# A six-layer cross network on one core: later loads issued layer by layer, the prologue's products reordered, one small weight load moved to GpSimd and small loads issued ahead of GpSimd's own work

## The chip, the cores and the metric

The kernel runs on one core of one Trainium2 chip. The metric is the device time of one execution in microseconds (us).

## The reference

The input x0 has 4096 rows and 416 columns (bf16); there are six layers, each with a 416x416 weight and a bias.

```python
B, F, D, L = 4096, 26, 16, 6          # Din = F * D = 416
def reference(x0, ws, bs):
    x = x0
    for l in range(ws.shape[0]):
        x = x0 * (x @ ws[l] + bs[l]) + x
    return x
```

Every layer multiplies by x0 and adds x. So x after l layers is x0 times a sum that can be kept in TensorE's accumulator banks: the kernel never clears them between layers, and adds a running sum of the biases ("bias sums").

## The kernel before

The 416 columns are three chunks of 128 and a tail of 32. The rows run in four blocks of 1024, the columns on the partitions, so x0 has to come in transposed. For the first block TensorE transposes most of it itself: rows 0 to 511 with transposes, rows 512 to 767 (the "third input block") and the 32 tail columns ("tail inputs") with products by an identity that GpSimd builds. Rows 768 to 1023 come by a transposing DMA. All of this is the prologue. Layer 0 of block 0 multiplies the first two chunks (k=0, k=1), then runs the third input block, the tail inputs and the bias sums, then k=2, and then the "tail rows": products whose contraction is the 32 tail columns, part 0 and part 1 (part 1 also uses the "corner" weights, tail columns by tail columns). After that each layer repeats the same pattern without any setup work.

Loads, and GpSimd's share:

```python
        IN_BANKS = ((3, 4, 6), (0, 5, 7))
        IN_ORDER = ((0, 0), (1, 0), (0, 1), (1, 1), (0, 2), (1, 2))
        THIRD = (6, 7, 3)
        HALVES = (slice(0, 64), slice(64, 128))
        # ... (cut)
        def load_wt(eng, g, a, b, done):
            n0, n1 = ((0, 256), (256, DF))[g % 2]
            eng.dma_start(
                wt_sb[lane(g), a:b, 0:n1 - n0], ws[a:b, DF:D, n0:n1].rearrange("l p n -> p l n")
            ).then_inc(done, 16)
        # ... (cut)
        @block.sync
        def _(sp):
            sp.dma_start(xin_sb[:, 0:2, :], x0_v[:, 0:2, :]).then_inc(s_xin[0], 16)
            sp.dma_start(w_sb[:, 0, 0, :], ws[0, 0:128, :]).then_inc(s_w0, 16)
            sp.dma_start(xin_sb[:, 4:6, :], x0_v[:, 4:6, :]).then_inc(s_xin[2], 16)
            load_wt(sp, 0, 0, 1, s_wt[0])
            sp.dma_start_transpose(x0T_sb[:, :, 768:SB], x0[768:SB, 0:DF]).then_inc(s_x0T[0], 16)
            for l in range(1, L):
                sp.dma_start(w_sb[:, l, :, :], wmain(l)).then_inc(s_w[l], 16)
                if l == 1:
                    for g in range(4):
                        load_wt(sp, g, 1, L, s_wt[1])
        # ... (cut)
            for s in range(1, NS):
                sp.dma_start_transpose(
                    x0T_sb[:, :, s * SB:(s + 1) * SB], x0[s * SB:(s + 1) * SB, 0:DF]
                ).then_inc(s_x0T[s], 16)
                sp.dma_start_transpose(
                    x4_sb[:, s - 1:s, :], x0[s * SB:(s + 1) * SB, D - 128:D]
                ).then_inc(s_x4[s - 1], 16)
            for s in range(NS - 1):
                n = (s + 1) * L
                sp.wait_ge(s_xa, NC * n)
                sp.wait_ge(s_xb, NC * n)
                for c in range(NC):
                    sp.dma_start_transpose(
                        o_sb[:, s * JS:(s + 1) * JS, c * 128:(c + 1) * 128], xo_sb[:, s, c, :]
                    ).then_inc(s_oT, 16)
                sp.wait_ge(s_xt, n)
                sp.dma_start_transpose(ot_sb[:, s, :, :], xot_sb[:, s, :]).then_inc(s_ot, 16)
                sp.wait_ge(s_oT, 16 * NC * (s + 1))
                sp.wait_ge(s_otc, s + 1)
                sp.dma_start(
                    out_v[:, s * JS:(s + 1) * JS, :], o_sb[:, s * JS:(s + 1) * JS, :]
                ).then_inc(s_out, 16)
        # ... (cut)
        @block.gpsimd
        def _(pool):
            pool.memset(ones_sb[:, :], 1.0).then_inc(s_ones, 1)
            pool.dma_start(bsa_sb[1:L + 1, :], bs[:, :]).then_inc(s_bs, 16)
            pool.wait_ge(s_ones, 1)
            pool.affine_select(
                out=ident[:, :], in_=ones_sb[:, 0:128], pattern=[[-1, 128]],
                compare_op=ALU.is_equal, fill=0.0, base=0, channel_multiplier=1,
            ).then_inc(s_set, 1)
            pool.affine_select(
                out=u_sb[:, :], in_=ones_sb[0:L + 1, 0:L], pattern=[[1, L]],
                compare_op=ALU.is_ge, fill=0.0, base=1, channel_multiplier=-1,
            ).then_inc(s_set, 1)
            load_wt(pool, 2, 0, 1, s_wtp)
            pool.wait_ge(s_zero, 1)
            for i, (a, b) in enumerate(((0, 1), (1, L))):
                for g in (1, 3):
                    pool.dma_start(
                        wc_sb[lane(g), a:b, 32 * g:32 * g + 32], ws[a:b, DF:D, DF:D].rearrange("l p n -> p l n")
                    ).then_inc(s_wc[i], 16)

        # ... (cut)
                    if l == 1 and s > 0:
                        pool.wait_ge(s_ot, 16 * s)
                        pool.tensor_copy(
                            out=o_sb[:, (s - 1) * JS:s * JS, DF:D].rearrange("p (g r) f -> p r g f", r=2),
                            in_=ot_sb[:, s - 1, :, :].rearrange("p r (g f) -> p r g f", f=DR),
                        ).then_inc(s_otc, 1)
        # ... (cut)
            def tail_inputs():
                for r in range(2):
                    for g in range(4):
                        for i in range(2):
                            j = 2 * (g ^ i) + r
                            src = xin_sb[:, j, DF:D] if j < 6 else xtl_sb[:, j - 6, :]
                            ins = tile_mm(ps[lane(g), 5 - i, r * 128:r * 128 + 128], src, ident[:, :], g, True)
                ins.then_inc(s_tp, 1)

            def third_input():
                pe.wait_ge(s_xin[2], 16)
                pe.wait_ge(s_inD, 4)
                for c in range(NC):
                    for j in range(2):
                        for q in range(4):
                            f0 = c * 128 + 32 * q
                            ins = tile_mm(
                                ps[lane(q), THIRD[c], j * 128:j * 128 + 128], xin_sb[:, 4 + j, f0:f0 + 32], ident[:, :], q, True
                            )
                    ins.then_inc(s_inT, 1)

            fill(14)
```

The order of the first layer on TensorE, and the copies out of its banks on VectorE (dve) and ScalarE (act):

```python
            def bias_sums():
                pe.wait_ge(s_bs, 16)
                pe.wait_ge(s_zero, 2)
                pe.wait_ge(s_set, 2)
                pe.wait_ge(s_inD, 5)
                for c in range(NC + 1):
                    for q in range(4):
                        f0 = c * 128 + 32 * q if c < NC else DF
                        ins = tile_mm(ps[lane(q), 6, c * 8:c * 8 + L], bsa_sb[:, f0:f0 + 32], u_sb[:, :], q, True)
                ins.then_inc(s_cbp, 1)
        # ... (cut)
                    if n == 0:
                        pe.wait_ge(s_w0, 16)
                        for k in range(NC):
                            if k == 1:
                                pe.wait_ge(s_w[0], 16)
                            if k == 2:
                                third_input()
                                pe.wait_ge(s_xtl0, 16)
                                tail_inputs()
                                bias_sums()
                            before_a(k)
                            for m in range(NC):
                                step(m, 0, k)
                    else:
                        if s == 0:
                            pe.wait_ge(s_w[l], 16)
                        chunk(0, 0, before_a)
                        chunk(1, 0)
                        chunk(2, 0)

                    if n == 0:
                        pe.wait_ge(s_inD, 6)
                        pe.wait_ge(s_inA, 3)
                        pe.wait_ge(s_te, 1)
                        pe.wait_ge(s_te0, 1)
                    else:
                        pe.wait_ge(s_xb, NC * n)
                        if l == 0:
                            pe.wait_ge(s_xt, n)
                            pe.wait_ge(s_te, s + 1)
                        else:
                            pe.wait_ge(s_sw, s * (L - 1) + l)
                    if s == 0 and l < 2:
                        if l == 1:
                            pe.wait_ge(s_wc[1], 32)
                        pe.wait_ge(s_wt[l], (48, 64)[l])
                    if n == 0:
                        pe.wait_ge(s_wtp, 16)

        # ... (cut)
                    lo, hi = slice(0, G), slice(G, 2 * G)
                    for part in range(2):
                        if n == 0 and part == 1:
                            pe.wait_ge(s_cb, 1)
                            pe.wait_ge(s_wc[0], 32)
                        for h in range(2):
                            g, wm = 2 * h, slice(part * 128, part * 128 + 128)
                            row(g, ps[:, NC * h + part, :], wt_sb[lane(g), l, wm], slice(0, H), h == 1)
                            g += 1
        # ... (cut)
                            else:
                                row(g, ps[:, 6 + h, lo], wc_sb[lane(g), l, 0:128], lo, True)
                        for h in range(2):
                            g = 2 * h + 1
                            if part == 1:
                                ins = row(g, ps[:, 6 + h, lo], wc_sb[lane(g), l, 32:160], hi, False)
                    ins.then_inc(s_ti, 1)
                    if n == 0:
                        pe.wait_ge(s_x0T[0], 16)
        # ... (cut)
            for c in (0, 2):
                dve.wait_ge(s_inT, 2 * NC + c + 1)
                dve.tensor_copy(out=x0T_sb[:, c, 512:768], in_=ps[:, THIRD[c], 0:G]).then_inc(s_inD, 1)
            dve.wait_ge(s_tp, 1)
            dve.tensor_copy(out=x0t_sb[:, 0, G:2 * G], in_=ps[:, 4, 0:G]).then_inc(s_te0, 1)
            dve.wait_ge(s_cb, 1)
        # ... (cut)
            act.wait_ge(s_inT, 2 * NC + 2)
            act.activation(out=x0T_sb[:, 1, 512:768], in_=ps[:, THIRD[1], 0:G], func=ACTF.Copy).then_inc(s_inA, 1)
            def swap_lanes(buf, done):
                for g in range(4):
                    ins = act.activation(out=buf[lane(g), G:2 * G], in_=buf[lane(g ^ 1), 0:G], func=ACTF.Copy)
                ins.then_inc(done, 1)

            act.wait_ge(s_tp, 1)
            act.activation(out=x0t_sb[:, 0, 0:G], in_=ps[:, 5, 0:G], func=ACTF.Copy).then_inc(s_te, 1)
            act.wait_ge(s_cbp, 1)
            act.activation(
                out=cb_sb[:, :, :],
                in_=ps[:, 6, 0:8 * (NC + 1)].rearrange("p (c e) -> p c e", e=8)[:, :, 0:L], func=ACTF.Copy,
            ).then_inc(s_cb, 1)
            act.wait_ge(s_cb, 1)
```

## Time and profile before

| | before |
|---|---|
| median device time | 130.58 us (3 runs, 130.36 to 130.84) |
| profiled span | 129.4 us |
| TensorE busy | 124.6 us, 96% |
| pitch of two layers in the chain of waits | 4.87 us, all 24 layers alike |
| layer 0's tail rows start (the end of the prologue) | 8.88 us |

In all lines of the profile PE is TensorE, PEld its weight loads, DVE VectorE, ACT ScalarE, POOL GpSimd and SP SyncE. L342 is source line 342, xN a count, and "issue" is time in which an engine waited for nothing that the profile shows.

From the chain of waits of before (start us, length us, what):

```profile
4.03 1.39 PE ps L240 x12
5.42 1.91 PE ps L201 x29
...
7.36 0.43 DVE x0T_sb L426
...
7.93 1.02 PE ps L201 x28
8.95 0.32 PE ps L342
...
9.49 4.33 PE ps L201 x84
```

Up to the end of the last layer the chain is TensorE's own work but for one piece: at 7.36 it is a VectorE copy. The piece of 4.33 us that starts at 9.49 is the body of layer 0, and it is followed by the next tail rows at 13.82, one layer pitch later.

From the timeline of before (start us, length us, engine, line, operation, and in brackets the idle time before it and what ended it):

```profile
1.38 0.72 POOL L159 DMA_DIRECT2D bsa_sb<-in_bs_dram  x1 [0.26 <-issue]
...
2.18 0.32 POOL L161 TENSOR_SCALAR_AFFINE_SELECT ident<-ones_sb 128x128 bf16<-128x128 bf16 x1
...
3.96 1.46 PE L240 MATMUL ps<-ident,xin_sb 128*128 128x128 bf16 x12
...
7.36 0.76 DVE L426 CAST x0T_sb<-ps 128x256 bf16<-128x256 f32 x2 [1.61 <-PE ps L201]
...
7.93 0.26 PE L201 MATMUL ps<-u_sb,bsa_sb 7*32 7x6 bf16 x16 [0.18 <-DVE x0T_sb L426]
...
8.88 0.39 PE L342 MATMUL ps<-x0t_sb,wt_sb 32*128 32x512 bf16 x1
...
9.42 2.45 PE L201 MATMUL ps<-x0T_sb,w_sb 128*32 128x256 bf16 x48
```

GpSimd starts the identity right after its first DMA issue, at 2.18. TensorE's bias sums stood still for 0.18 us because they write bank 6, from which VectorE was still copying the third input block.

### The profile page before, as it was taken

The page shows a single profiled execution, that of the slowest core. Times are in us where ns is not written, and L with a number is a line of the kernel's source. Part 1 is how long each engine was busy: PE and PEld are TensorE (multiplying, and loading weights), DVE is VectorE, ACT ScalarE, POOL GpSimd, SP SyncE. Part 2 cuts the span into 40 slices and gives each one's busy share as a digit, 9 for nine tenths or more (in the row PEclk, how much of TensorE's full clock was granted, in tenths as well). Part 3 has the DMA queues.
Part 4 walks back from the last instruction along what each step waited for, and adds up shares of the span by engine and source line. Part 5 has one row for each costly group of instructions (what it writes and reads, how often), then busy time and mean ns, then how long its engine had stood idle before and what let it go on. Part 6 is the DMA issues. An engine that isn't in the chain of part 4 may idle for free.

```text
span 129.4 us, 5407 instructions
## 1 busy us (share of the span) xinstructions
PE 124.6 (96%) x2448; PEld 62.7 (48%) x2448; DVE 100.3 (78%) x154; ACT 71.4 (55%) x164; POOL 22.7 (18%) x41
## 2 busy tenths in 40 slices
PE   7999999999999999999999999999999999999980
PEld 6655445445445445445445445445445445445450
DVE  2339779779779779779779779779789789789790
ACT  0626456476746456475745555575755555555680
POOL 7602012012012022012012022022022032022130
PEclk9999999999999999999999999999999999999999
DMA  3999999898007708000008944000009834000025
GB/s 107 295 264 318 124 194 174 177 120 181 0 10 126 143 0 268 0 0 5 5 0 159 110 136 133 5 0 0 5 0 115 154 129 139 5 0 5 0 85 186
DMA packets 32934, 12.54 MB, mean 97 GB/s; under 512 B 25338, under 2 KB 32912, under 8 KB 32912
## 3 DMA queue, kind: packets, MB, share of 16 engines
q1 hardware_dynamic: 31536, 11.49, 44.0%
q10 hardware_dynamic: 1184, 0.67, 1.7%
q8 instruction: 19, 0.31, 1.0%
q0 software_dynamic: 192, 0.05, 0.2%
q14 instruction: 3, 0.02, 0.1%
HBM read 2.90 MB, written 3.41 MB: 49 GB/s over the span
## 4 chain that ended last, share of the span: by engine, by line
PE 96%; DVE 1%; issue 0%; DVEq 0%
PE ps L201 84%; PE ps L342 10%; PE ps L240 1%; DVE o_sb L451 1%; PE ps L395 0%; DVE x0T_sb L426 0%; DVEq L33 0%; PE ps L357 0%
## 5 line engine op out<-in xcount | busy, mean ns | idle before, releaser
L446 DVE SCALAR_TENSOR_TENSOR xT_sb<-ps,cb_sb,x0T_sb 128x512 bf16<-128x512 f32 x120 | 80.9, 743 | 16.9 <-PE ps L342 16.9
L201 PE MATMUL ps<-xT_sb,w_sb 128*32 128x512 bf16 (+1 forms) x1680 | 89.0, 364 | 0.0
L201 PEld LDWEIGHTS ps<-xT_sb,w_sb 128*32 128x32 bf16 x1680 | 43.0, 97 | 38.7 <-issue 4.2
L475 ACT ACTIVATE xt_sb<-xt_sb 32x256 bf16<-32x256 bf16 x80 | 33.1, 414 | 16.6 <-POOL xt_sb L188 15.9
L498 ACT ACTIVATE t_sb<-ps,cb_sb 64x256 f32<-64x256 f32 x48 | 22.5, 469 | 30.5 <-PE ps L201 30.2
L188 POOL TENSOR_TENSOR xt_sb<-t_sb,x0t_sb 128x256 bf16<-128x256 f32 x20 | 13.4, 672 | 83.0 <-ACT t_sb L498 83.0
L201 PE MATMUL ps<-x0T_sb,w_sb 128*32 128x512 bf16 (+1 forms) x336 | 18.8, 369 | 0.0
L446 DVE SCALAR_TENSOR_TENSOR xo_sb<-ps,cb_sb,x0T_sb 128x512 bf16<-128x512 f32 x23 | 15.6, 744 | 3.4 <-PE ps L342 3.3
L201 PEld LDWEIGHTS ps<-x0T_sb,w_sb 128*32 128x32 bf16 x336 | 8.5, 98 | 7.9 <-issue 1.6
L342 PE MATMUL ps<-xt_sb,wt_sb 32*128 32x512 bf16 x80 | 12.1, 379 | 0.0
L511 ACT ACTIVATE x0t_sb<-x_sb 32x256 bf16<-32x256 bf16 x24 | 9.9, 413 | 0.4
L357 PE MATMUL ps<-xt_sb,wt_sb 32*128 32x512 bf16 x40 | 7.8, 385 | 0.0
L342 PE MATMUL ps<-xt_sb,wc_sb 32*128 32x256 bf16 x80 | 7.7, 268 | 0.0
L342 PEld LDWEIGHTS ps<-xt_sb,wt_sb 32*128 32x128 bf16 x80 | 2.3, 92 | 8.5 <-DVE xT_sb L446 8.5
L342 PEld LDWEIGHTS ps<-xt_sb,wc_sb 32*128 32x128 bf16 x80 | 4.0, 93 | 2.3
L188 POOL TENSOR_TENSOR xot_sb<-t_sb,x0t_sb 128x256 bf16<-128x256 f32 x4 | 2.7, 671 | 12.6 <-ACT t_sb L498 12.6
L201 PE MATMUL ps<-const-bfloat16-1.0 128*32 128x256 bf16 x56 | 3.2, 419 | 0.8 <-PEq L548 0.8
L421 DVE COPY x0T_sb<-ps 128x256 bf16<-128x256 bf16 x4 | 1.0, 292 | 2.9 <-PE ps L240 2.9
L468 ACT ACT_TABLE_LOAD x1 | 1.3, 1283 | 3.4 <-issue 3.4
L201 PEld LDWEIGHTS ps<-const-bfloat16-1.0 128*32 128x32 bf16 x56 | 2.4, 144 | 1.2 <-issue 0.8
L342 PE MATMUL ps<-x0t_sb,wt_sb 32*128 32x512 bf16 x16 | 2.4, 380 | 0.0
L173 POOL DMA_DIRECT2D wc_sb<-in_ws_dram x4 | 2.2, 554 | 0.0
(45 smaller groups left out, 28.8 us busy)
## 6 DMA issues: line engine op xcount, KB each, us to landing
out_dram<-o_sb SPq DMA_DIRECT2D x3, 832.0 KB, 4.1
w_sb<-in_ws_dram SPq DMA_DIRECT2D x5, 312.0 KB, 4.5
xin_sb<-in_x_dram SPq DMA_DIRECT2D x2, 208.0 KB, 3.5
out_dram<-o_sb SPq DMA_DIRECT2D x1, 256.0 KB, 2.3
xin_sb<-in_x_dram ACTq DMA_DIRECT2D x1, 208.0 KB, 3.2
w_sb<-in_ws_dram ACTq DMA_DIRECT2D x1, 208.0 KB, 3.9
out_dram<-o_sb SPq DMA_DIRECT2D x1, 208.0 KB, 2.3
out_dram<-o_sb ACTq DMA_DIRECT2D x1, 208.0 KB, 2.7
```

Of the source, the lines that this page charges most:

```text
L173: pool.dma_start(wc_sb[lane(g), a:b, 32 * g:32 * g + 32], ws[a:b, DF:D, DF:D].rearrange("l p n -> p l n")).then_inc(s_wc[i], 16)
L188: pool.tensor_tensor(out=dst, in0=t32_sb[:, n % 2, :], in1=x0t_sb[:, s, 0:G], op=ALU.mult).then_inc(s_xt, 1)
L201: return pe.matmul(dst, lhsT=lhsT, rhs=rhs, start=start, stop=True, skip_group_check=True, tile_position=(0, 32 * q),)
L240: ins = pe.transpose(out=psT[:, IN_BANKS[h][c], (j % 2) * 128:(j % 2 + 1) * 128], in_=xin_sb[:, j, c * 128:(c + 1) * 128], identity=ident[ ...
L342: return pe.matmul(dst, lhsT=lhsT, rhs=srct[lane(g), cols], start=l == 0 and start, stop=True, skip_group_check=True, tile_position=(32 * ...
L357: pe.matmul(ps[:, NC * h + 2, :], lhsT=wt_sb[lane(g), l, 0:128], rhs=srct[lane(g), :].rearrange("p (b r) -> p b r", b=2)[:, ::-1, :], star ...
L446: dve.scalar_tensor_tensor(out=dst, in0=ps[:, NC * half + c, :], scalar=cb_sb[:, c, l:l + 1], in1=x0T_sb[:, c, o:o + H], op0=ALU.add, op1= ...
L451: dve.tensor_copy(out=o_sb[:, j0 + 4:j0 + 8, 0:256], in_=psT[:, 4, :].rearrange("p (j d) -> p j d", d=256)).then_inc(s_oeD, 1)
L468: act.activation(out=x0T_sb[:, 1, h * 256:(h + 1) * 256], in_=psT[:, IN_BANKS[h][1], 0:256], func=ACTF.Copy).then_inc(s_inA, 1)
L475: ins = act.activation(out=buf[lane(g), G:2 * G], in_=buf[lane(g ^ 1), 0:G], func=ACTF.Copy)
L498: ins = act.activation(out=t32_sb[HALVES[h], n % 2, :], in_=tail(h), func=ACTF.Identity, bias=cb_sb[HALVES[h], NC, l:l + 1],)
L511: ins = act.activation(out=x0t_sb[lane(g), s + 1, swap * G:(swap + 1) * G], in_=x4_sb[96:128, s, r * G:(r + 1) * G], func=ACTF.Copy,)
```

## The change

It has four intents. (1) The bias sums go into bank 4, which is free, so that they need not wait. (2) The tail inputs go ahead of the third input block, both halves into one bank, so that one ScalarE copy replaces a ScalarE and a VectorE copy; the copy of the bias sums goes from ScalarE to VectorE, and some waits of the first tail rows move to part 1. (3) One tail weight moves from SyncE to GpSimd, and GpSimd issues it, the other tail weight and one corner weight before it builds the identity. (4) Weights of layers 2 to 5 are issued as the layers proceed, and the transposed rows of later blocks one block at a time.

```diff
-        THIRD = (6, 7, 3)
+        THIRD = (3, 6, 7)
# ... (cut)
 
         @block.sync
         def _(sp):
+            def load_rows(s):
+                sp.dma_start_transpose(
+                    x4_sb[:, s - 1:s, :], x0[s * SB:(s + 1) * SB, D - 128:D]
+                ).then_inc(s_x4[s - 1], 16)
+                sp.dma_start_transpose(
+                    x0T_sb[:, :, s * SB:(s + 1) * SB], x0[s * SB:(s + 1) * SB, 0:DF]
+                ).then_inc(s_x0T[s], 16)
+
             sp.dma_start(xin_sb[:, 0:2, :], x0_v[:, 0:2, :]).then_inc(s_xin[0], 16)
             sp.dma_start(w_sb[:, 0, 0, :], ws[0, 0:128, :]).then_inc(s_w0, 16)
             sp.dma_start(xin_sb[:, 4:6, :], x0_v[:, 4:6, :]).then_inc(s_xin[2], 16)
-            load_wt(sp, 0, 0, 1, s_wt[0])
             sp.dma_start_transpose(x0T_sb[:, :, 768:SB], x0[768:SB, 0:DF]).then_inc(s_x0T[0], 16)
             for l in range(1, L):
+                if l > 1:
+                    sp.wait_ge(s_ti, (1, 2, 2, 2)[l - 2])
+                if l == L - 1:
+                    load_rows(1)
                 sp.dma_start(w_sb[:, l, :, :], wmain(l)).then_inc(s_w[l], 16)
                 if l == 1:
                     for g in range(4):
                         load_wt(sp, g, 1, L, s_wt[1])
-            for s in range(1, NS):
-                sp.dma_start_transpose(
-                    x0T_sb[:, :, s * SB:(s + 1) * SB], x0[s * SB:(s + 1) * SB, 0:DF]
-                ).then_inc(s_x0T[s], 16)
-                sp.dma_start_transpose(
-                    x4_sb[:, s - 1:s, :], x0[s * SB:(s + 1) * SB, D - 128:D]
-                ).then_inc(s_x4[s - 1], 16)
             for s in range(NS - 1):
                 n = (s + 1) * L
                 sp.wait_ge(s_xa, NC * n)
@@ -137,6 +141,8 @@
                     ).then_inc(s_oT, 16)
                 sp.wait_ge(s_xt, n)
                 sp.dma_start_transpose(ot_sb[:, s, :, :], xot_sb[:, s, :]).then_inc(s_ot, 16)
+                if s < NS - 2:
+                    load_rows(s + 2)
                 sp.wait_ge(s_oT, 16 * NC * (s + 1))
                 sp.wait_ge(s_otc, s + 1)
                 sp.dma_start(
@@ -157,6 +163,16 @@
         def _(pool):
             pool.memset(ones_sb[:, :], 1.0).then_inc(s_ones, 1)
             pool.dma_start(bsa_sb[1:L + 1, :], bs[:, :]).then_inc(s_bs, 16)
+            for g in (0, 2):
+                load_wt(pool, g, 0, 1, s_wtp)
+            def load_wc(i, g):
+                a, b = ((0, 1), (1, L))[i]
+                pool.dma_start(
+                    wc_sb[lane(g), a:b, 32 * g:32 * g + 32], ws[a:b, DF:D, DF:D].rearrange("l p n -> p l n")
+                ).then_inc(s_wc[i], 16)
+
+            pool.wait_ge(s_zero, 1)
+            load_wc(0, 1)
             pool.wait_ge(s_ones, 1)
             pool.affine_select(
                 out=ident[:, :], in_=ones_sb[:, 0:128], pattern=[[-1, 128]],
@@ -166,13 +182,9 @@
                 out=u_sb[:, :], in_=ones_sb[0:L + 1, 0:L], pattern=[[1, L]],
                 compare_op=ALU.is_ge, fill=0.0, base=1, channel_multiplier=-1,
             ).then_inc(s_set, 1)
-            load_wt(pool, 2, 0, 1, s_wtp)
-            pool.wait_ge(s_zero, 1)
-            for i, (a, b) in enumerate(((0, 1), (1, L))):
-                for g in (1, 3):
-                    pool.dma_start(
-                        wc_sb[lane(g), a:b, 32 * g:32 * g + 32], ws[a:b, DF:D, DF:D].rearrange("l p n -> p l n")
-                    ).then_inc(s_wc[i], 16)
+            load_wc(0, 3)
+            for g in (1, 3):
+                load_wc(1, g)
 
             for s in range(NS):
# ... (cut: the copy of the stored tail moves from layer 1 to layer 2 of the next row block)
                             j = 2 * (g ^ i) + r
                             src = xin_sb[:, j, DF:D] if j < 6 else xtl_sb[:, j - 6, :]
-                            ins = tile_mm(ps[lane(g), 5 - i, r * 128:r * 128 + 128], src, ident[:, :], g, True)
+                            ins = tile_mm(ps[lane(g), 5, i * G + r * 128:i * G + r * 128 + 128], src, ident[:, :], g, True)
                 ins.then_inc(s_tp, 1)
 
             def third_input():
-                pe.wait_ge(s_xin[2], 16)
# ... (cut)
                 pe.wait_ge(s_bs, 16)
                 pe.wait_ge(s_zero, 2)
                 pe.wait_ge(s_set, 2)
-                pe.wait_ge(s_inD, 5)
                 for c in range(NC + 1):
                     for q in range(4):
                         f0 = c * 128 + 32 * q if c < NC else DF
-                        ins = tile_mm(ps[lane(q), 6, c * 8:c * 8 + L], bsa_sb[:, f0:f0 + 32], u_sb[:, :], q, True)
+                        ins = tile_mm(ps[lane(q), 4, c * 8:c * 8 + L], bsa_sb[:, f0:f0 + 32], u_sb[:, :], q, True)
                 ins.then_inc(s_cbp, 1)
# ... (cut)
                             if k == 1:
                                 pe.wait_ge(s_w[0], 16)
                             if k == 2:
-                                third_input()
+                                bias_sums()
+                                pe.wait_ge(s_xin[2], 16)
                                 pe.wait_ge(s_xtl0, 16)
                                 tail_inputs()
-                                bias_sums()
+                                third_input()
                             before_a(k)
                             for m in range(NC):
                                 step(m, 0, k)
@@ -320,10 +331,9 @@
                         chunk(2, 0)
 
                     if n == 0:
-                        pe.wait_ge(s_inD, 6)
-                        pe.wait_ge(s_inA, 3)
+                        pe.wait_ge(s_inD, 5)
                         pe.wait_ge(s_te, 1)
-                        pe.wait_ge(s_te0, 1)
+                        pe.wait_ge(s_cb, 1)
                     else:
                         pe.wait_ge(s_xb, NC * n)
                         if l == 0:
@@ -334,9 +344,9 @@
                     if s == 0 and l < 2:
                         if l == 1:
                             pe.wait_ge(s_wc[1], 32)
-                        pe.wait_ge(s_wt[l], (48, 64)[l])
+                        pe.wait_ge(s_wt[l], (32, 64)[l])
                     if n == 0:
-                        pe.wait_ge(s_wtp, 16)
+                        pe.wait_ge(s_wtp, 32)
# ... (cut)
                     lo, hi = slice(0, G), slice(G, 2 * G)
                     for part in range(2):
                         if n == 0 and part == 1:
-                            pe.wait_ge(s_cb, 1)
+                            pe.wait_ge(s_inD, 6)
+                            pe.wait_ge(s_inA, 3)
                             pe.wait_ge(s_wc[0], 32)
# ... (cut)
+            dve.wait_ge(s_cbp, 1)
+            dve.tensor_copy(
+                out=cb_sb[:, :, :], in_=ps[:, 4, 0:8 * (NC + 1)].rearrange("p (c e) -> p c e", e=8)[:, :, 0:L],
+            ).then_inc(s_cb, 1)
             for c in (0, 2):
                 dve.wait_ge(s_inT, 2 * NC + c + 1)
                 dve.tensor_copy(out=x0T_sb[:, c, 512:768], in_=ps[:, THIRD[c], 0:G]).then_inc(s_inD, 1)
-            dve.wait_ge(s_tp, 1)
-            dve.tensor_copy(out=x0t_sb[:, 0, G:2 * G], in_=ps[:, 4, 0:G]).then_inc(s_te0, 1)
             dve.wait_ge(s_cb, 1)
# ... (cut)
-            act.wait_ge(s_inT, 2 * NC + 2)
-            act.activation(out=x0T_sb[:, 1, 512:768], in_=ps[:, THIRD[1], 0:G], func=ACTF.Copy).then_inc(s_inA, 1)
             def swap_lanes(buf, done):
                 for g in range(4):
                     ins = act.activation(out=buf[lane(g), G:2 * G], in_=buf[lane(g ^ 1), 0:G], func=ACTF.Copy)
                 ins.then_inc(done, 1)
 
             act.wait_ge(s_tp, 1)
-            act.activation(out=x0t_sb[:, 0, 0:G], in_=ps[:, 5, 0:G], func=ACTF.Copy).then_inc(s_te, 1)
-            act.wait_ge(s_cbp, 1)
-            act.activation(
-                out=cb_sb[:, :, :],
-                in_=ps[:, 6, 0:8 * (NC + 1)].rearrange("p (c e) -> p c e", e=8)[:, :, 0:L], func=ACTF.Copy,
-            ).then_inc(s_cb, 1)
+            act.activation(out=x0t_sb[:, 0, :], in_=ps[:, 5, :], func=ACTF.Copy).then_inc(s_te, 1)
+            act.wait_ge(s_inT, 2 * NC + 2)
+            act.activation(out=x0T_sb[:, 1, 512:768], in_=ps[:, THIRD[1], 0:G], func=ACTF.Copy).then_inc(s_inA, 1)
             act.wait_ge(s_cb, 1)
```

## The prediction

> **What bounds the kernel now.** The page gives TensorE busy 124.6 of 129.4 us (96%); the chain of waits is TensorE for 96%. In that chain successive layers' tail-row groups start 4.87 us apart, all 24 layers (13.82, 18.69, 23.56 ... 121.00), in stretches with a DMA share of 1.25 as of 0.15 (windows view). The steady state is pure matmul work and no load is late there. Only the prologue, before the first tail rows at 8.88 us, can move. The end is untouched.
>
> **Prologue, from the timeline and the trace's landing records.** Warm-up fill 0.85 to 4.03; transposes from 3.96; layer-0 products k=0,1 5.42 to 7.0; third input block and tail inputs 7.02 to 7.75; then TensorE waits for VectorE's copy (7.36 to 7.74) because the bias sums reuse bank 6; bias sums 7.93; k=2 8.12; tail rows 8.88. The bubble is 0.18 us of empty TensorE. Landings: first input 3.70, second 3.99, tail of rows 768-1023 6.78, tail weights 7.57, corner weights 7.77, transposed block 8.13: none ends a wait.
>
> **What the change does.**
> 1. Bias sums move to bank 4, already free: the bubble vanishes, -0.2 us on the critical path.
> 2. Tail inputs first, both halves in one bank, one ScalarE copy 128x512 (estimate 0.69 us, from the 128x512 a32 copy; it replaces 0.38 on ScalarE and 0.42 on VectorE in parallel). ScalarE should end it about 8.6 and its third-block copy about 9.0; part 1 of the tail rows waits for that. No saving; up to 0.1 us lost.
> 3. Tail weights on GpSimd, ahead of the identity. GpSimd issues cost 0.72, 0.60 and 0.55 us each and occupy it in order: before, the identity starts only at 2.18, after the bias issue (1.38 to 2.10). Now two tail-weight issues and one corner issue also precede it: it ends near 4.25 instead of 2.50, and the transposes start near 4.3 instead of 3.96: +0.3 us on the critical path. The Trainium skill ("DMA: Bandwidth & Descriptors", section SWDGE vs HWDGE vs iDMA) says software on GpSimd writes these descriptors; the durations agree. Part comes back: TensorE still runs slow there (fill weight loads 144 ns against 97 later, first products up to 609 ns against 379), until about 6.1 us. The skill ("TensorE: Matmul & The Clock Gate", Part 1) ascribes this to a free-running activity window; if the speed-up comes at the same time, fewer later products run slow, and the net cost is about +0.15.
> 4. Layer-by-layer loads, transposes spread between outputs, tail copy a layer later: 0. Layer-5 weights should land near 27 us and are needed at 31. SyncE's queue waits, TensorE doesn't.
>
> Sum: -0.2 + 0.15 (0.3 at worst) + 0 to 0.1: about -0.05 us, sign open.
>
> **Prediction: 130.5 us, 80% range 130.0 to 131.0.** Faster by over 2%: 0.01. Within 2%: 0.98. Slower by over 2%: 0.01.
>
> **What would show it right.** Layer pitch stays 4.87 us. Identity ends near 4.25, transposes start with it. The bias sums' wait for VectorE is gone. Layer 0's tail rows start at 8.7 to 8.95. The DMA share falls between 8 and 20 us without effect on TensorE. If the identity isn't late, step 3 is wrong and 0.2 to 0.3 us are gained.
>
> **What would make it wrong.** The gap before the transposes delays the clock's release by a window (over 1 us lost); corner weights, now issued last near 4.4, land after 9.05; layer-5 weights, queued behind the transposes, arrive late; the constant pitch hides a cost of the early DMA flood.

## More of the kernel before

The profiled span of an execution is 1.7 to 1.9 us shorter than its device time, in every run that lists both.

From the page of before: the span, the busy times by engine, DMA activity in 40 slices of 3.2 us (tenths), the queue that carries instructions (packets, MB, share), and the engines' shares of the chain of work that ended last.

```profile
span 129.4 us, 5407 instructions
...
PE 124.6 (96%) x2448; PEld 62.7 (48%) x2448; DVE 100.3 (78%) x154; ACT 71.4 (55%) x164; POOL 22.7 (18%) x41
...
DMA  3999999898007708000008944000009834000025
...
q8 instruction: 19, 0.31, 1.0%
...
PE 96%; DVE 1%; issue 0%; DVEq 0%
```

TensorE is the chain. The slices from about 6 to 30 us have the DMA engines busy nearly all the time, because everything for the later layers and blocks is issued at once.

## The result, and the profile after

| | before | after |
|---|---|---|
| median device time | 130.43 us (6 runs, 130.22 to 130.84) | 130.62 us (6 runs, 130.49 to 130.95) |
| ratio | | 1.0017, 95% interval 0.9997 to 1.0037 |
| profiled span | 129.4 us | 129.1 us |
| transposes start | 3.96 us | 4.11 us |
| layer 0's tail rows start | 8.88 us | 8.63 us |

A ratio is the mean time of one kernel's runs over that of the other's runs of the same rounds, so it is not quite the ratio of the medians in the table. Executions over 1.5% slower than the fastest of the same kernel are left out of the means.

The page of after, same lines:

```profile
span 129.1 us, 5404 instructions
...
PE 124.4 (96%) x2448; PEld 62.7 (49%) x2448; DVE 100.2 (78%) x154; ACT 71.4 (55%) x163; POOL 23.2 (18%) x42
...
DMA  3974199400008698800008987800009700700026
...
PE 94%; POOL 2%; DVE 1%; issue 0%; DVEq 0%; POOLq 0%
```

The DMA row is emptier between 6 and 30 us, and TensorE's share of the chain fell from 96% to 94%, with GpSimd in it now.

The chain of waits of after:

```profile
2.10 1.07 POOL wt_sb L107 x2
...
3.74 0.32 POOL ident L177
...
4.11 1.46 PE ps L251 x12
5.57 3.12 PE ps L213 x90
8.70 0.32 PE ps L352
...
9.24 4.33 PE ps L213 x84
```

VectorE's piece is gone. In its place the chain starts with GpSimd's issues of the tail weights and with the identity. The timeline of after:

```profile
2.09 1.08 POOL L107 DMA_DIRECT2D wt_sb<-in_ws_dram  x2
...
3.16 0.50 POOL L170 DMA_DIRECT2D wc_sb<-in_ws_dram  x1
...
3.74 0.31 POOL L177 TENSOR_SCALAR_AFFINE_SELECT ident<-ones_sb 128x128 bf16<-128x128 bf16 x1
...
4.11 1.46 PE L251 MATMUL ps<-ident,xin_sb 128*128 128x128 bf16 x12
...
7.11 0.26 PE L213 MATMUL ps<-u_sb,bsa_sb 7*32 7x6 bf16 x16
...
7.78 0.60 ACT L490 ACTIVATE x0t_sb<-ps 128x512 bf16<-128x512 f32 x1 [2.15 <-PE ps L213]
...
8.63 0.38 PE L352 MATMUL ps<-x0t_sb,wt_sb 32*128 32x512 bf16 x1
...
9.17 2.45 PE L213 MATMUL ps<-x0T_sb,w_sb 128*32 128x256 bf16 x48
```

The identity ran at 3.74 instead of 2.18 and TensorE's transposes started with it, 0.15 us later than before. The bias sums follow the first products without a gap. The tail rows start 0.25 us earlier.

So the profiles show a gain of 0.26 us in the span, and the timed runs show no gain. The two have to be brought together first.

### A confounder: the moment at which TensorE's clock is released

Each trace has a record of the granted clock. In the profile of before full clock is on record from 6.12 us, in that of after from 5.95 us. Both records last 122.88 us and are followed by half clock. The Trainium skill ("TensorE: Matmul & The Clock Gate", Part 1) describes a free-running window of 3413 ns that decides between half and full clock; 122.88 us is 36 such windows. (The record lasts 122.88 us in 12 of the 14 traces, and 126.29 us, 37 windows, in e4 and e8.) Work ahead of that moment runs at about half speed: in before, groups of four like products of layer 0 start 0.40 us apart ahead of 6.12 and 0.21 us apart after it. The moment differs from run to run.

Every run lists its span S and its mean granted clock c. Since the clock is on record as half only after the release plus 122.88 us, the release can be estimated for a run as S x (1 - 2(1 - c)) - 122.88. This works where c is below 1; with c of 1.000 the drop came after the end, and the release can have been late or early: in the profiles of e4 and e8 (c = 1.000) it was at 4.68 and 4.31, and full clock lasted a window longer. For the profiles it gives the recorded release to about 0.2 us; c is listed to 0.001, which alone is 0.26 us of release. With 42 such runs of before, a straight line fits: S = 126.97 + 0.392 x release, with a scatter of 0.07 us. The estimates run from 3.8 to 6.5 us and the spans from 128.5 to 129.6. **The same kernel moves by 1.1 us through the draw of the release, four times the effect in question.** Comparisons below are therefore made at the same release where they can be.

A second regularity helps to read the traces. In all traces but two, the span minus the start of layer 0's body in the chain of waits (9.49 in before, 9.24 in after) is 119.87 to 119.89 us. Whatever the change does, it has to do it before that point. The two exceptions are e8, by 0.03 us, and e11, by more than 1 us, which is told below.

### The profile page after: what moved, and what is told of

Read it like the earlier page. It is cut to its first block, busy times and chain, and to the rows that moved or that the text cites. A ratio compares the mean times of both kernels' runs of the same rounds, so it can differ in the third digit from the quotient of the medians.

```text
span 129.1 us, 5404 instructions
## 1 busy us (share of the span) xinstructions
PE 124.4 (96%) x2448; PEld 62.7 (49%) x2448; DVE 100.2 (78%) x154; ACT 71.4 (55%) x163; POOL 23.2 (18%) x42
## 4 chain that ended last, share of the span: by engine, by line
PE 94%; POOL 2%; DVE 1%; issue 0%; DVEq 0%; POOLq 0%
PE ps L213 82%; PE ps L352 10%; PE ps L251 1%; POOL wt_sb L107 1%; POOL bsa_sb L165 1%; DVE o_sb L464 1%; PE ps L406 0%; POOL wc_sb L170 0%; POOL ident L177 0%; POOL ones_sb L164 0%; DVEq L33 0%; PE ps L368 0%; POOLq L177 0%; POOLq L556 0%
## 5 line engine op out<-in xcount | busy, mean ns | idle before, releaser
L213 PE MATMUL ps<-x0T_sb,w_sb 128*32 128x512 bf16 (+1 forms) x336 | 18.7, 367 | 0.0
```

Source lines behind the costliest of these rows:

```text
L213: return pe.matmul(dst, lhsT=lhsT, rhs=rhs, start=start, stop=True, skip_group_check=True, tile_position=(0, 32 * q),)
```

## The experiments

Theory: the reordering (1 and 2) saves about 0.2 us, and the GpSimd part (3) takes it back, by the late identity and by corner weights that land late; the load schedule (4) is worth nothing. Rivals: the reordering saves nothing; or the load schedule costs something; or the difference is only the draw of the release.

### e1: the kernel before, again

No edit.

> The kernel before against itself. Both theories (the change is worth a saving of about 0.2 us in the prologue; the change is worth nothing or costs 0.2 us) expect a ratio of 1.000. What counts is the spread: if the spans follow the moment at which TensorE's clock is released (6.12 us in the first profile), the runs should scatter by 0.3 to 0.6 us with the granted clock figure moving with the span, and that scatter is then as large as the whole effect of the change. If the scatter is under 0.1 us, the 0.19 us between the medians of after and before is real.

Measured: 130.77 us against 130.53, ratio 1.0015 (0.998 to 1.005). Its six spans were 128.6, 128.7, 128.9, 129.0, 129.5 and 129.6 at estimated releases of 3.9, 4.5, 5.0, 5.35, 6.4 and 6.5. The kernel differs from itself by as much as the changed kernel differs from it, and the spans follow the release.

### e2 and e12: the changed kernel, again

No edit.

> The changed kernel once more, on the chip of the other runs. Theory A (profile is right: tail rows of layer 0 start 0.26 us earlier, of which about 0.1 is a luckier clock release): ratio 0.998 to 0.9995. Rival B (the timed medians are right and something outside the prologue costs): ratio 1.001 to 1.003 with the layer pitch still 4.87 us and a later end.

> The changed kernel a third time. Theory: spans at a release of 5.9 to 6.0 are 129.1 (0.25 under before), at 5.4 are 128.9 to 129.1 (level with before), at 4.5 and earlier are 128.8 to 128.9 (0.1 to 0.3 over before), because the corner weights land at 8.4 to 8.6 whatever the clock does; ratio over all runs 0.999 to 1.002. Rival (no dependence on the release): a constant difference to before over all releases.

Measured: e2 130.88 against 130.53, ratio 1.0017 (0.9989 to 1.0045); e12 130.73 (five runs) against 130.56, ratio 1.0014 (0.9997 to 1.0031). e2's ratio lies in rival B's range, but not for rival B's reason: the pitch is 4.87 us and nothing is lost after the prologue. With the first six runs there are 17, of which 14 allow an estimate of the release. Against the line of before at the same release they are:

| estimated release | runs of after | span minus the line of before |
|---|---|---|
| 5.6 and later | 5 | -0.17 to -0.21 us |
| 4.6 to 5.6 | 8 | 0.00 to -0.25, mean -0.10 us |
| below 4.6 | 1 | +0.28 us |

So the changed kernel gains about 0.2 us at a late release, less at an early one, and its one early run lost. That is the dependence e12's theory asked for, though its early branch rests on a single run. Only one of 14 estimates lies below 4.6, against 15 of 42 for before. Whether the late identity pushes early releases into a later window, or this is chance, is open.

The profile of e2 (release 5.38) shows where the gain goes. Its release is the same as that of e7 (5.39), whose compute and GpSimd parts are those of before. First e2, then e7, from their timelines:

```profile
8.39 0.38 PE L352 MATMUL ps<-x0t_sb,wt_sb 32*128 32x512 bf16 x1
...
8.74 0.09 PEld L352 LDWEIGHTS ps<-x0t_sb,wt_sb 32*128 32x128 bf16 x1 [0.25 <-issue]
...
9.10 2.45 PE L213 MATMUL ps<-x0T_sb,w_sb 128*32 128x256 bf16 x48
```

```profile
8.52 0.38 PE L349 MATMUL ps<-x0t_sb,wt_sb 32*128 32x512 bf16 x1
...
9.06 2.45 PE L208 MATMUL ps<-x0T_sb,w_sb 128*32 128x256 bf16 x48
```

Tail rows start 0.13 us earlier in e2 (8.39 against 8.52). But part 1 of them, 8.74, had stood for 0.25 us, where nothing on the engines released it: the trace's landing record has the last corner weight at 8.63. The body of layer 0 starts at 9.10 against 9.06, so the gain is gone. In the first profile of after the corner weights had landed at 8.39, just ahead of tail rows that a late clock had put at 8.63, and nothing was lost.

### e3: identity first

```diff
             pool.dma_start(bsa_sb[1:L + 1, :], bs[:, :]).then_inc(s_bs, 16)
+            # wait for ones; affine_select ident; affine_select u  (moved up)
             for g in (0, 2):
                 load_wt(pool, g, 0, 1, s_wtp)
             ...
             load_wc(0, 1)
-            # wait for ones; affine_select ident; affine_select u
             load_wc(0, 3)
```

> The changed kernel with the identity built before the tail weights are issued, as in before. Step 3 of the prediction right (the late identity holds the transposes back): the transposes start at 3.9 to 4.0 instead of 4.11 and layer 0's tail rows at about 8.5 instead of 8.62, 0.1 us faster than the changed kernel. Rival (the transposes wait for the end of the warm-up fill or for the first input, not for the identity): they start at 4.1 again and nothing moves. Tail weights should land at 7.0 to 7.4 as before, since only 0.5 us of GpSimd work moves ahead of them.

Measured: 130.67 against 130.53, ratio 1.0005 (0.9973 to 1.0037). From its timeline (release 4.37):

```profile
3.96 1.02 PE L251 MATMUL ps<-ident,xin_sb 128*128 128x128 bf16 x12
...
8.02 0.38 PE L352 MATMUL ps<-x0t_sb,wt_sb 32*128 32x512 bf16 x1
...
8.51 0.09 PEld L352 LDWEIGHTS ps<-x0t_sb,wt_sb 32*128 32x128 bf16 x1 [0.40 <-issue]
...
8.87 2.45 PE L213 MATMUL ps<-x0T_sb,w_sb 128*32 128x256 bf16 x48
```

The transposes start at 3.96 again, so they had waited for the identity: that half of the expectation held. The tail rows start at 8.02. But part 1 again waits, 0.40 us in the weight loads, for corner weights that landed at 8.41. With two tail weights and both corner weights of layer 0 on GpSimd, the last of them lands at 8.4 to 8.6 in after, e2, e3 and e12, whether the identity comes first or not (8.10 in e6); with one tail weight fewer (before, e1, e7) it landed at 7.4 to 7.8. Against the line of before, e3's three runs with an estimate are at +0.12 and +0.05 us (releases of 4.37 and 4.28) and at -0.27 us (5.86): the same dependence on the release as in the changed kernel, which gives its early branch two more runs.

### e4 and e8: identity still later, without and with work for TensorE in the gap

```diff
 # e4, against the changed kernel
+            load_wc(0, 3)
+            load_wc(1, 1)
             # wait for ones; affine_select ident; affine_select u
-            load_wc(0, 3)
-            for g in (1, 3):
-                load_wc(1, g)
+            load_wc(1, 3)
 # e8, against e4
-            fill(14)
+            fill(19)
```

> The changed kernel with two more corner-weight issues (0.55 us each) ahead of the identity. Step 3 right: the identity ends at about 5.15, the transposes start at 5.2 (1.1 us later than in the changed kernel), and layer 0's tail rows start at 9.2 to 9.5, since the part of the work that then falls after the clock's release runs at double rate: 0.6 to 0.9 us slower than the changed kernel, ratio to before about 1.005. If the gap in TensorE's work delays the release by a whole window, over 1.5 us slower. Rival (slack hides the identity): under 0.2 us.

> The kernel with the identity 1.1 us later, whose runs fell in two groups (spans 129.6 and 130.9 to 131.4), with 5 more groups of warm-up products so that TensorE has work until the identity is there. Theory (an idle gap of 1.2 us in the clock monitor's window makes it miss the release by a whole window in four of six runs): the slow group disappears, all runs at 131.2 to 131.8, spans under 130. Rival (the spread comes from something else, such as late weights): two groups again, up to 133.

Measured: e4 132.79 against 130.53, ratio 1.0139 (1.0087 to 1.0191); its spans were 129.6 twice and 130.9 to 131.4 four times. The profile fell among the fast ones:

```profile
5.20 0.84 PE L251 MATMUL ps<-ident,xin_sb 128*128 128x128 bf16 x12 [1.17 <-POOL ident L179]
```

The wait for the identity is on the critical path, without any slack. The transposes moved from 4.11 to 5.20, by 1.09 us. In the chain of waits the body of layer 0 starts at 9.71, against 9.24 in after. That looks as if half of the delay had been given back, but e4's clock was released at 4.68 and after's at 5.95, and by the slope above 1.27 us of release are worth about 0.5 us. So at equal release 0.9 to 0.95 us of the 1.09 is lost (an estimate: the slope is that of before, and the changed kernel, by the table above, gains a little less from an early release). The clock hands little back, which is not what the prediction assumed. e8 came to 131.65 against 130.68, ratio 1.0102 (1.0064 to 1.0140), with spans of 129.6 to 129.9 four times and 131.0 and 131.1 twice. The slow group shrank from four of six to two of six and did not disappear, so the theory that the gap alone causes it is not confirmed. The distance between the groups, 1.3 to 1.8 us in e4 and 1.1 to 1.5 in e8, is near the 1.3 us that a release one window later would cost by the slope above (an estimate), so a missed window stays a candidate. No profile caught a slow run; what makes them slow stays open.

### e5: the GpSimd part undone

```diff
 # SyncE, against the changed kernel
             sp.dma_start(xin_sb[:, 4:6, :], x0_v[:, 4:6, :]).then_inc(s_xin[2], 16)
+            load_wt(sp, 0, 0, 1, s_wt[0])
 # GpSimd: as in the kernel before (identity, one tail weight, both corner weights)
```

> The changed kernel with its GpSimd part undone: one tail weight issued by SyncE again, identity built first, both corner weights issued right after the one tail weight that GpSimd had. Theory (GpSimd part eats what the reordering gains, by the late identity, 0.15 us, and by the corner weights landing at 8.4 to 8.6 instead of 7.6 to 7.8): transposes start at 3.96, corner weights land by 7.8, part 1 of layer 0's tail rows follows part 0 after 0.2 to 0.25 us, tail rows start about 0.25 us earlier than in before at the same clock release (about 8.0 at a release near 4.4); time 0.15 to 0.3 us under before, ratio 0.998. Rival (the reordering itself gains nothing): ratio 1.000 or above.

Measured: 130.57 against 130.68, ratio 0.9992 (0.9969 to 1.0015). Corner weights landed at 7.67 and part 1 followed part 0 without a wait. Against the line of before its runs were at -0.23, -0.21, -0.01, +0.24 and +0.44 us. From its timeline (release 4.02):

```profile
6.34 0.26 PE L208 MATMUL ps<-u_sb,bsa_sb 7*32 7x6 bf16 x16
...
6.70 0.13 PEld L208 LDWEIGHTS ps<-ident,xin_sb 128*32 128x32 bf16 x4 [0.20 <-issue]
...
8.06 0.38 PE L347 MATMUL ps<-x0t_sb,wt_sb 32*128 32x512 bf16 x1
```

At so early a release TensorE reaches the tail inputs before their last load has landed: the load of the tail of rows 768 to 1023 landed at 6.59, and the tail inputs stood for 0.2 us (in the weight-load row). Before, the third input block ran first and covered that wait. So, measured at equal release, e5 is ahead of before in two runs and behind in two, and no version faster than before by a clear margin has been found. Why two early runs had spans of 129.0 is not settled, as neither was profiled.

### e6: the GpSimd part alone

```diff
 # the kernel before, with GpSimd's and SyncE's load_wt/load_wc/affine_select order of the change,
 # and the two wait counts that go with it
-                        pe.wait_ge(s_wt[l], (48, 64)[l])
+                        pe.wait_ge(s_wt[l], (32, 64)[l])
-                        pe.wait_ge(s_wtp, 16)
+                        pe.wait_ge(s_wtp, 32)
```

> The kernel before with the GpSimd part alone. Theory: transposes start at 4.11 instead of 3.96, corner weights land at 8.4 to 8.6; since here the tail rows start later than in the changed kernel the corner weights hardly hold them; cost 0.1 to 0.25 us, ratio 1.001 to 1.002. Rival (GpSimd part harmless): the same as before, 1.000, with the transposes at 3.96.

Measured: 131.48 against 130.68, ratio 1.0052 (1.0029 to 1.0075). The part costs, more than expected. In the profile the transposes start at 4.10, the corner weights land at 8.10, too early to be waited for. Against the line of before, two runs at a late release (6.6) are +0.16 us, which fits the late identity. Two at an early one (4.4 and 4.25) are +0.40 and +0.56; these were not profiled, and what they waited for is open. (e11 below gives a candidate, the fetching of instructions: e6 too has the loads of before.)

### e7: the load schedule alone

```diff
 # the kernel before, with SyncE's loop of the change
             for l in range(1, L):
+                if l > 1:
+                    sp.wait_ge(s_ti, (1, 2, 2, 2)[l - 2])
+                if l == L - 1:
+                    load_rows(1)
                 sp.dma_start(w_sb[:, l, :, :], wmain(l)).then_inc(s_w[l], 16)
 # ... rows of blocks 2 and 3 between the stores; tail copy in layer 2
```

> The kernel before with the load schedule alone (weights layer by layer, transposed rows between outputs, tail copy a layer later). Theory (step 4 is worth nothing): ratio 1.000, layer pitch 4.87 us, DMA share 10 to 20 us halved, no new waits of TensorE. Rival (the loads' traffic slows the prologue or the stores, or the late loads hold a layer): ratio off by 0.002 or more, or a layer pitch that differs from 4.87 in the layers where the loads fall (around 20 to 25, 47 to 51, 76 to 82 us).

Measured: 130.99 against 130.68, ratio 1.0033 (1.0006 to 1.0061). Taken alone this interval says slower. The runs drew late releases, though: five estimates lie at 4.8 to 6.3 us, and against the line of before they are at -0.15, -0.11, -0.07, -0.02 and +0.26, mean -0.02. The pitch is 4.87 us in every layer. Alone, the schedule moves nothing, as predicted.

### e9: the small load ahead of the large one

```diff
 # ScalarE, against e5
+            act.dma_start(xtl_sb[:, :, :], x0_v[:, 6:JS, DF:D]).then_inc(s_xtl0, 16)
             act.dma_start(w_sb[:, 0, 1:NC, :], ...).then_inc(s_w[0], 16)
-            act.dma_start(xtl_sb[:, :, :], x0_v[:, 6:JS, DF:D]).then_inc(s_xtl0, 16)
```

> The version with the GpSimd part undone, and the 16 KB load of the tail of rows 768 to 1023 issued ahead of the 208 KB layer-0 weights on ScalarE's queue. Theory (at an early clock release TensorE reaches the tail inputs at 6.5 us, before that load has landed, 6.04 to 6.78 in the traces so far): the load lands before 5.5, the gap of 0.18 us between bias sums and tail inputs is gone, tail rows start at 7.9 for a release near 4 (8.06 without), the layer-0 weights still land before 5.45; time 0.2 to 0.35 us under before, ratio 0.9975 to 0.9985, and no runs at an early release with spans of 129.0. Rival (those slow early-release runs come from elsewhere): the spans spread as they did, 128.4 to 129.1, ratio 0.999.

Measured: 131.34 against 130.76, ratio 1.0044 (1.0014 to 1.0075). A miss. The small load did land early, at 4.64. But the 208 KB of layer-0 weights, issued 0.5 us later, landed at 6.76 instead of 4.87 to 5.82 as in the other traces (median about 5.0), and TensorE stood still for them. Swapping the two loads did this; which property of the small one (16 KB in rows of 64 bytes) delays the large one was not tested. The chain of waits of e9, its first two long pieces:

```profile
1.87 4.89 DMA w_sb<-in_ws_dram
...
6.80 2.35 PE ps L208 x80
```

A DMA is the head of the chain here, which it is in no other trace.

### e10: the third input block first again

First an edit was built that changes nothing but the bank of the bias sums in the kernel before (columns 256 and up of bank 4). It was rejected before it could run: the bias sums and VectorE's copy of the tail inputs would use one bank at the same time, with nothing to order them. So with the bias sums in bank 4, part 1 of the change can't be tried without the tail inputs' new layout. The order can:

```diff
 # against e5
                                 bias_sums()
                                 pe.wait_ge(s_xin[2], 16)
+                                third_input()
                                 pe.wait_ge(s_xtl0, 16)
                                 tail_inputs()
-                                third_input()
 # ScalarE: the third block's copy ahead of the tail copy
```

> The version with the GpSimd part undone, and the third input block again ahead of the tail inputs, bias sums first in the freed bank, one tail copy after the third block's copy on ScalarE. Theory (putting the tail inputs first only moved the wait for their late load forward by the 0.35 us that the third block takes): no gap before the tail inputs at an early release, but the tail copy (0.60) now ends last and holds the tail rows for about 0.1 to 0.2 us, so tail rows at 8.0 to 8.1 for a release near 4 and 0.1 us later than with tail inputs first at a late release; ratio 0.998 to 0.9995. Rival (tail inputs first was worth a saving of its own): slower than before by 0.1 us or more.

Measured: 130.64 against 130.76, ratio 1.001 (0.9974 to 1.0046). Against the line of before the runs are at -0.13 to +0.08, mean +0.01. The wait for the late load is gone, and the tail copy now holds the tail rows: it ended at 7.93, the last of the copies, and their weight loads began at 7.99 (after 0.59 us idle, against 0.42 elsewhere). With this order the gain at a late release is gone (+0.04 us in the one run released after 6.0, against -0.17 to -0.21 for the changed kernel and -0.21 for e5), so tail inputs first was worth something there, as the rival said, though on one run. It also means that the free bank by itself saves nothing: e10 has it.

### e11: the reordering alone

```diff
 # e5 with SyncE's loads and the layer of the tail copy as in the kernel before
```

> The kernel before with the reordering alone: bias sums in the freed bank, tail inputs first with one copy; loads and GpSimd as in before. Theory (the reordering saves about 0.2 us at a late clock release, about 0.1 or less at an early one where it waits for the tail rows' load): spans lie 0.15 to 0.25 us under those of before at the same release (before: 128.7 at 4.5, 129.0 at 5.35, 129.4 at 6.0, 129.5 at 6.4), with now and then an early-release run that is not faster; ratio 0.9975 to 0.9995, whatever the draw of the releases adds. Rival (it needs the new load schedule to gain): on the line of before.

Measured: 131.68 against 130.56, ratio 1.0075 (1.0043 to 1.0106). The theory missed by a whole microsecond, in the wrong direction. Against the line of before its five runs with an estimate are at +0.34 to +0.77 us. Against e5 only the load schedule and the layer of the tail copy differ; e5 was timed against before on its own chip. From the chain of waits of e11 (release 5.28):

```profile
8.89 4.48 PE ps L201 x84
13.38 0.32 PE ps L340
...
13.92 4.32 PE ps L201 x81
18.24 0.53 issue
18.77 0.40 PE ps L201 x3
19.16 0.32 PE ps L340
...
19.71 4.33 PE ps L201 x84
```

The prologue did what was expected: layer 0's body starts at 8.89 in the chain of waits, where e7's (release 5.39) starts at 9.13. Of these 0.24 us the release is worth 0.04, so the reordering saved 0.2 us here. But layer 0 takes 5.03 us instead of 4.87, and layer 1 takes 5.78, with 0.53 us in which TensorE waited for nothing that the profile shows. The span lies 120.95 us behind the start of layer 0's body, not 119.88: 1.07 us are lost after the prologue, 0.16 in layer 0 and 0.91 in layer 1.

What it waited for can be narrowed. The trace has 19 transfers of 16384 bytes on the instruction queue. TensorE's program has 2448 products, each of which becomes a weight load and a product, and TensorE stopped twice, until 11.25 and until 18.77, here in its weight loads:

```profile
11.25 1.63 PEld L201 LDWEIGHTS ps<-xT_sb,w_sb 128*32 128x32 bf16 x35 [0.27 <-issue]
...
18.77 0.10 PEld L201 LDWEIGHTS ps<-xT_sb,w_sb 128*32 128x32 bf16 x2 [1.02 <-issue]
```

Between the two stops lie 255 or 256 of its instructions in program order. The Trainium skill ("Runtime: NRT & Kernel Launch", section "Instruction fetch mechanics") says that instructions are fetched in blocks of 16 KiB, 256 instructions, while the engine executes the current one, and that the cost is "mostly hidden". The transfer ahead of the first stop ended at 9.76, that ahead of the second at 17.19: each stop ended 1.5 to 1.6 us after it. Other traces have the first of these stops too, too short to cost anything but 0.04 us in layer 0 of e8: in e2, e3 and e12 the same weight load as in e11 (the 220th of the program) came 0.06 to 0.17 us after the one before it (in the remaining traces there is no such gap), in e8 the next one 0.25 us after, and each time this was 1.44 to 1.48 us after the end of the first transfer. No trace passes that place sooner after the transfer than 1.44 us. By this reading TensorE stood at the end of what had been fetched. The start of that second transfer, from the trace's transfer records:

| load schedule | traces | second instruction transfer starts |
|---|---|---|
| all at once | before, e1 | 12.75, 13.19 us |
| all at once | e6, e11 | 15.27, 16.21 us |
| layer by layer | after, e2, e3, e4, e5, e7, e8, e9, e10, e12 | 11.32 to 12.63 us |

With the loads issued at once, the second fetch comes later in all four traces than in any of the ten others. In before it ended at 14.5; adding the 1.5 us seen in e11, it was usable at about 16.0 (an estimate), and TensorE needed it only near 18.7, which is 14.37 plus the 4.32 us that e11 ran in that layer. In e11 it came 3.5 us later and TensorE 0.45 us earlier. That the fetches are what TensorE waited for is inferred from the block length, from the equal delays and from the common place in the program; no run here changed the fetching itself. Why the second fetch starts at 16.2 in e11 and at 12.75 in before, with the same loads, is open.

## Why the prediction was right

The forecast was 130.5 us, within 2%; measured 130.62. The sum of small terms of both signs came out as said, in part by luck, and a forecast of no change tests the terms little: even e4, with the identity a microsecond late, is within 2% of before (ratio 1.0139). Term by term:

- **Steady state fixed, only the prologue can move.** Right for this change: the distance from layer 0's body to the end is 119.88 us before and after. It isn't a law, as e11 shows: the same compute order with the old loads loses 1.07 us after the prologue.
- **Bias sums in the free bank, -0.2 us.** Right that the wait for VectorE (0.18 us) goes: it is gone in every trace that has the new bank. At a late release the whole change is 0.17 to 0.21 us under before. But the saving is not the bank's alone: e10 has the bank and gains nothing, so it takes the bank together with the tail inputs first.
- **One tail copy, up to 0.1 us lost.** The copy took 0.60 us, not the estimated 0.69, and no trace of the changed kernel waits for it. The tail rows' weight loads wait for the usual 0.42 us. That the step is what lets the bank's saving through (e10) wasn't in the prediction, and neither was what it did cost: with the tail inputs first, an early release meets their late load (0.2 us in e5).
- **The late identity, +0.3 us on the start, +0.15 net.** Right in kind and in net size, by two errors that cancel. The transposes started 0.15 us later, not 0.3: the identity ended at 4.06, not 4.25, because three issues on GpSimd took 1.58 us (1.08 for the two tail weights, 0.50 for the corner weight) where 1.75 was added up. And the half that the clock was to give back was not seen: e6, with a start 0.14 later than before, lost 0.16 us at a late release, and e4 0.9 to 0.95 of 1.09 (an estimate). The Trainium skill ("DMA: Bandwidth & Descriptors", section "SWDGE vs HWDGE vs iDMA") has these descriptors computed by software on GpSimd; the trace agrees in that its own work waits behind them; that software is the reason isn't shown, since SyncE's and ScalarE's issues of plain loads take 0.43 to 0.57 us each too.
- **Corner weights.** Listed as a risk for the case that they land after 9.05. They land earlier than that, at 8.4 to 8.6, but tail rows at an early release need them earlier too; they cost 0.15 us in e2 and 0.3 us in e3. The prediction took one release of the clock, that of its profile, for all runs.
- **Load schedule 0.** Right for the kernel before (e7), and wrong as a statement about the changed kernel. Layer 5's weights landed at 25.2 us, ahead of the forecast 27. In the changed kernel it is worth 1.07 us by the two profiles (e5 against e11, with ratios of 0.9992 and 1.0075 to before), and about 0.6 us by the means of their runs against the line of before (+0.05 and +0.62): without it the reordering would have made the kernel slower. "The constant pitch hides a cost of the early DMA flood" was named among the risks, and that is what the runs showed, by all signs in the fetching of instructions.

What remains is the timed excess of the changed kernel, about 0.2 us in three sets of runs (ratios 1.0017, 1.0017 and 1.0014), each with an interval that holds 1. Its 14 runs at a known release lie 0.11 us under the line of before on average, and their mean span is that of the 42 runs of before, 128.96 us both, because they drew later releases (5.3 against 5.1 in the mean). So the excess comes from the runs with c of 1.000, whose release is unknown: eight of before with a mean span of 128.7, three of after with 129.2. Whether the change makes early releases rarer or this is chance is not settled.

## What to carry to other kernels

Before explaining a few tenths of a microsecond, find what scatters the runs of one and the same kernel, and compare at equal values of it; here the clock's release alone spans 1.1 us and made an interval for a neutral change exclude 1. Small loads aren't free by being moved to another queue: GpSimd's own work waits behind each issue, the last in line lands late, and a 16 KB load put ahead of a 208 KB one delayed it by about 1.8 us, of which 0.5 us is its later issue. A part of a change that is worth nothing alone can be what makes the rest of it possible, so test parts both alone and taken away from the whole.

## What the Trainium skill lacked or had wrong

- "Runtime: NRT & Kernel Launch", section "Instruction fetch mechanics": the cost of a block boundary is given as "mostly hidden". With the loads issued at once, TensorE stopped at two places 255 or 256 instructions apart, by the reading above two such boundaries, and the kernel lost 1.07 us in all (e11); 1.44 to 1.58 us passed between the end of a block's transfer and TensorE going on (e2, e3, e8, e11, e12). The page doesn't say how data traffic delays the fetch.
- "DMA: Bandwidth & Descriptors", section "Anatomy of one DMA": descriptor generation on GpSimd is called "small, variable". Here each small issue (2 to 16 KB) held GpSimd for about 0.5 to 0.72 us, and other GpSimd work waited for it.
- The same page, section "Issuing engines are not separate DMA queues", says that all queues share the engines. It gives no figure for what a load of many 64-byte rows costs a large one behind it: with 16 KB ahead of 208 KB on one queue, the large one landed at 6.76 instead of 4.9 to 5.8 us (e9).
- "TensorE: Matmul & The Clock Gate", Part 1: the free-running window is described, and it fits (122.88 us is 36 windows, and the 126.29 us of e4 and e8 are 37). That the mean granted clock and the span of a run give its release, so that runs can be compared at equal release, is on no page; the slope here is 0.39 us of span for each us of release.
